# A decode kernel's output written as two single-row transfers on two queues, and its MLP bias loaded in two pieces

## The chip, the cores and the metric

The kernel runs on one core of a Trainium2 chip. The metric is the device time of one execution in microseconds (us); before the change the median of three runs is 134.12 us. Profiles show one execution each; their span (132.1 us here) is counted from the first to the last instruction and is a little shorter than the device time.

## The reference

One decoding step for two sequences (B = 2, one token each, width 576): attention over a window of the last 2048 cached positions, and beside it an MLP with squared ReLU. Both start from the same layer-normed input, and both are added to the input. The MLP's own x is not used.

```python
def _A_ref(x, k_cache, v_cache, wq, wo):          # 32 query heads, 16 KV heads, head size 128
    W = min(4096, max(256, Sk // 4))              # 2048 of 8192 positions
    q = (x @ wq).reshape(B, Sq, Hq, Dh)...
    k = jnp.repeat(k_cache[:, :, Sk - W:, :], rep, axis=1)
    v = jnp.repeat(v_cache[:, :, Sk - W:, :], rep, axis=1)
    p = _softmax(jnp.einsum("bhqd,bhkd->bhqk", q, k) * (Dh ** -0.5))
    o = jnp.einsum("bhqk,bhkd->bhqd", p, v)
    return o... @ wo                              # 4096 -> 576

def _B_ref(x, w1, b1, w2, b2):                    # 576 -> 4608 -> 576
    h = jnp.einsum("bsd,df->bsf", x, w1) + b1
    r = jnp.where(h > 0, h, 0)
    return jnp.einsum("bsf,fd->bsd", r * r, w2) + b2

xn = _layernorm(A_x)
return A_x + _A_ref(xn, ...) + _B_ref(xn, ...)    # (2, 1, 576), bf16
```

## The kernel before

The sync engine's queue loads K, V and all large weights, one transfer after another. The scalar engine's queue loads the input x, the two biases, and writes the output. All that is to be summed (input, second bias, attention times wo, MLP times w2) is accumulated by matmuls in one PSUM tile, `out_ps`. The 576 columns of the result stand there as four quarters of 144 columns, quarter q of sequence b on partition 32 q + 16 b, which gives eight partitions with data.

```python
    BS = 16
    MB = BS * (B - 1) + 1                # 17
    RM = 32 * (NG4 - 1) + MB             # 113
    OQ = D // 4                          # 144
    W2P = [(9, 15), (15, 17), (17, 18)]  # pieces of the last part of w2
    R9 = 9
    HW = L1 // NG4                       # 576
    ...
    xb_sb = const.tile([B + 1, D], BF16, name="xb_sb")
    nc.scalar.dma_start(out=x_sb, in_=x2d)
    ...
    load_k(0)                            # all on the sync queue
    wq_sb = issue_flat(A_wq, "wq")
    load_k(1); load_v(0); load_k(2); load_v(1); load_k(3)   # one per line in the kernel
    ...
    b1_sb = const.tile([2 * NG4, HW], BF16, name="b1_sb")   # 8 rows of 576
    ...
    softmax(0)
    load_v(2)
    b1_rows = B_b1.rearrange("(x n) -> x n", n=HW)
    for i0, i1 in ((0, 2), (2, 4), (4, 6), (6, 8)):
        nc.scalar.dma_start(out=b1_sb[i0:i1, :], in_=b1_rows[i0:i1, :])
    nc.scalar.dma_start(out=xb_sb[B:B + 1, :], in_=B_b2.rearrange("(o n) -> o n", o=1))
    step(1)
    ...
    mlp_h(w1_sb)                         # uses b1_sb
    wo_sb = issue_flat(A_wo, "wo")
    ...
    nc.sync.dma_start(out=w2a_sb[:], in_=w2_rows[0])
    nc.sync.dma_start(out=w2b_sb[:], in_=w2_rows[1, :, 0:R9 * D])
    for r0, r1 in W2P:
        nc.sync.dma_start(out=w2c_sb[:, (r0 - R9) * D:(r1 - R9) * D], in_=w2_rows[1, :, r0 * D:r1 * D])
    step(NU - 1)
    pv_all(NU - 2)
    pv_all(NU - 1)
    ...                                  # out_ps += wo, w2a parts
    for r in range(FR):                  # FR = 18
        w, o = (w2b_sb, r) if r < R9 else (w2c_sb, r - R9)
        out_acc(hT_sb[:, 1, r, :], w, o, stop=(r == FR - 1))

    fin_sb = work.tile([RM, OQ], BF16, tag="fin", name="fin_sb")
    out_v = out2d.rearrange("b (q n) -> q b n", q=4)
    nc.scalar.dma_start(out=out_v, in_=w2b_sb[0:RM:BS, 0:OQ])   # early, of no meaning
    nc.scalar.copy(out=fin_sb[:], in_=out_ps[:])
    nc.scalar.dma_start(out=out_v, in_=fin_sb[0:RM:BS, :])      # the output
```

The first of the two output transfers writes weights, which the second overwrites. It serves to have a transfer of this form run once before the one that counts. The framework orders the two by a semaphore.

Of the kernel before, what the change touches and what calls it, by code (L numbers as in the profile page):

```python
# [16 lines left out]
def kernel(  # L17
# [14 lines left out]
    nc = tc.nc  # L32
    P = 128
    B, Sq, D = A_x.shape
# [43 lines left out]
    BS = 16  # L78
    MB = BS * (B - 1) + 1
    RM = 32 * (NG4 - 1) + MB  # L80
    OQ = D // 4
# [18 lines left out]
    out2d = out.rearrange("b s d -> (b s) d")  # L100
# [79 lines left out]
    for t0, half, k0, n, pc in ((0, 0, 0, NK, 0), (0, 1, 0, NK, 1), (1, 0, 1, NK - 1, 1), (1, 1, 0, NK - 1, 0)):  # L180
# [11 lines left out]
                          in_=own[:].unsqueeze(2).to_broadcast([P, NC, WC]))  # L192
# [11 lines left out]
                          in_=ident[0:2 * NG4, 0:2 * NG4].rearrange("p (x g) -> p x g", g=NG4).unsqueeze(3)  # L204
# [209 lines left out]
    softmax(0)  # L414
    load_v(2)
    b1_rows = B_b1.rearrange("(x n) -> x n", n=HW)
    for i0, i1 in ((0, 2), (2, 4), (4, 6), (6, 8)):
        nc.scalar.dma_start(out=b1_sb[i0:i1, :], in_=b1_rows[i0:i1, :])
    nc.scalar.dma_start(out=xb_sb[B:B + 1, :], in_=B_b2.rearrange("(o n) -> o n", o=1))
    step(1)  # L420
# [16 lines left out]
    w2b_sb = kvpool.tile([P, R9 * D], BF16, tag="kv", name="w2b")  # L437
# [13 lines left out]
        out_acc(hT_sb[:, 1, r, :], w, o, stop=(r == FR - 1))  # L451

    fin_sb = work.tile([RM, OQ], BF16, tag="fin", name="fin_sb")
    out_v = out2d.rearrange("b (q n) -> q b n", q=4)
    nc.scalar.dma_start(out=out_v, in_=w2b_sb[0:RM:BS, 0:OQ])
    nc.scalar.copy(out=fin_sb[:], in_=out_ps[:])  # L456
    nc.scalar.dma_start(out=out_v, in_=fin_sb[0:RM:BS, :])


# [28 lines left out]
```

## Time and profile before

| | us |
|---|---|
| device time, median of 3 runs (133.97 to 134.12) | 134.12 |
| span of the profiled execution | 132.1 |
| TensorE matmul busy | 84.6 (64%) |
| VectorE busy | 63.2 (48%) |
| ScalarE busy | 46.7 (35%) |
| bytes read from memory | 53.62 MB, 406 GB/s over the span |

How to read it: busy shares are of the whole span. An engine at 64% can still wait most of the time in one stage and be the limit in another, so the stages are what counts. "PEld" is TensorE's weight load, "ACTq" and "SPq" are the queues on which the scalar and the sync engine issue transfers, and `L457` is a line of the kernel. The time of an issuing instruction is not the transfer's time: the transfer starts after it and has landed when its semaphore has all its increments.

The DMA queues of the whole execution (packets, bytes, share of the 16 DMA engines' time), of which q1 is the sync engine's and q10 the scalar engine's, and the small transfers that this change is about:

```profile
q1 hardware_dynamic: 3456, 53.61, 95.2%
q10 hardware_dynamic: 46, 0.02, 0.1%
...
b_sb<-in_B_b_dram ACTq DMA_DIRECT2D x4, 2.2 KB
...
out_dram<-w2b ACTq DMA_DIRECT2D x1, 2.2 KB
out_dram<-fin_sb ACTq DMA_DIRECT2D x1, 2.2 KB
```

### The profile page before, as it was taken

How to read it: one execution, taken by the hardware profiler on the slowest of the kernel's cores; microseconds unless marked ns; L12 is line 12 of the kernel's file. 1: busy time of each engine (PE TensorE's matmuls, PEld its weight loads, DVE VectorE, ACT ScalarE, POOL GpSimd, SP SyncE). 2: the span in 40 equal slices, each digit the busy share in tenths (PEclk: the TensorE clock that was granted, in tenths of full speed). 3: DMA queues.
4: the chain of work that ended last, by engine and by line, in shares of the span. 5: the costliest groups of instructions: out<-in, count | busy, mean ns of one | idle time of the engine just before them, and what ended most of it. 6: DMA issues, size and time to landing. Idle time of an engine off the chain costs nothing.

```text
span 132.1 us, 2285 instructions
## 1 busy us (share of the span) xinstructions
PE 84.6 (64%) x949; PEld 52.6 (40%) x949; DVE 63.2 (48%) x176; ACT 46.7 (35%) x67; POOL 4.9 (4%) x15
## 2 busy tenths in 40 slices
PE   0089319599589687697599787104819972739471
PEld 0069202286345353363455443002417640229360
DVE  7764400344557677396547687410075667550000
ACT  5725400339566085283256094200106632000000
POOL 5000000010010100100100100100000001000000
PEclk9999955959999999999779999855695999555955
DMA  4999899999999999999999999999999999899960
GB/s 160 397 437 526 369 388 442 422 432 432 429 432 422 442 417 427 437 432 437 432 427 414 437 488 402 445 424 405 427 427 442 468 435 458 376 408 418 418 255 1
DMA packets 3511, 53.76 MB, mean 407 GB/s; under 512 B 419, under 2 KB 558, under 8 KB 814
## 3 DMA queue, kind: packets, MB, share of 16 engines
q1 hardware_dynamic: 3456, 53.61, 95.2%
q8 instruction: 7, 0.11, 0.3%
q10 hardware_dynamic: 46, 0.02, 0.1%
q14 instruction: 2, 0.02, 0.0%
HBM read 53.62 MB, written 0.00 MB: 406 GB/s over the span
## 4 chain that ended last, share of the span: by engine, by line
DMA 78%; PE 15%; ACT 2%; SPq 1%; DVE 1%; issue 1%; ACTq 0%; DVEq 0%
DMA w<-in_B_w_dram 25%; DMA w2c<-in_B_w_dram 24%; DMA k<-in_A_k_cache_dram 16%; DMA wq<-in_A_wq_dram 13%; PE kT_ps L97 5%; PE h_ps L94 3%; PE q_ps L94 3%; PE sc_ps L94 2%; PE out_ps L94 1%; PE o_ps L94 1%; ACT kT L270 1%; DVE qrow L238 1%; SPq L106 0%; ACT qrow L238 0%; DVE qz L254 0%
## 5 line engine op out<-in xcount | busy, mean ns | idle before, releaser
L97 PE MATMUL kT_ps<-ident_f,k 128*128 128x128 f32 x256 | 41.4, 312 | 5.7 <-DMA k<-in_A_k_cache_dram 3.9
L97 PEld LDWEIGHTS kT_ps<-ident_f,k 128*128 128x128 f32 x256 | 32.9, 161 | 18.8 <-issue 9.9
L270 ACT COPY kT<-kT_ps 128x1024 bf16<-128x1024 bf16 x32 | 31.9, 1012 | 17.8 <-PE kT_ps L97 17.8
L272 DVE COPY kT<-kT_ps 128x1024 bf16<-128x1024 bf16 x32 | 21.8, 682 | 6.4 <-PE kT_ps L97 6.1
L94 PE MATMUL sc_ps<-kT,qz 128*32 128x512 bf16 x128 | 9.9, 388 | 6.7 <-DVE kT L272 4.7
L302 ACT ACTIVATE p<-sc_ps,bias 128x512 bf16<-128x512 f32 x8 | 5.5, 688 | 21.4 <-DVE gown L298 18.2
L94 PE MATMUL o_ps<-v,pT 128*32 128x512 bf16 x128 | 11.2, 429 | 0.0
L94 PEld LDWEIGHTS <-xnT 128*4 128x4 bf16 x108 | 3.5, 121 | 16.8 <-issue 15.2
L94 PE MATMUL h_ps<-w,xnT 128*4 128x288 bf16 x72 | 4.3, 429 | 8.0 <-DMA w<-in_B_w_dram 8.0
L305 DVE STREAM_TRANSPOSE pT<-p 128x512 bf16<-128x512 bf16 x8 | 5.7, 710 | 6.2 <-ACT p L302 6.2
L335 DVE SCALAR_TENSOR_TENSOR o<-o_ps,in_s,o 128x128 f32<-128x128 f32 x24 | 8.3, 345 | 0.4
L291 DVE TENSOR_REDUCE m<-sc_ps 128x1 f32<-128x512 f32 x8 | 5.5, 692 | 4.8 <-PE sc_ps L94 4.8
L375 DVE TENSOR_TENSOR hrow<-t 100x1152 bf16<-100x1152 f32 x2 | 2.6, 1355 | 9.6 <-ACT t L373 9.6
L94 PE MATMUL q_ps<-wq,xnT 128*4 128x512 bf16 x36 | 4.0, 627 | 4.9 <-DMA wq<-in_A_wq_dram 4.9
L295 POOL PARTITION_ALL_REDUCE gmax<-m x8 | 2.9, 367 | 104.9 <-DVE m L293 104.9
L94 PE MATMUL op_ps<-o,of_h 128*32 128x129 f32 x16 | 3.7, 316 | 4.6 <-DVE o L335 4.6
L456 ACT CAST fin_sb<-out_ps 113x144 bf16<-113x144 f32 x1 | 0.3, 280 | 17.9 <-PE out_ps L94 17.9
L94 PEld LDWEIGHTS <-qz 128*32 128x32 bf16 x128 | 2.1, 94 | 10.4 <-DVE kT L272 7.2
L97 PE MATMUL pro_ps<-ident,xn_sb 2*128 2x2 bf16 x5 | 0.9, 182 | 6.8 <-DVE xn_sb L171 6.5
L94 PEld LDWEIGHTS <-hT_sb 128*17 128x17 bf16 x144 | 3.4, 108 | 3.6 <-issue 3.5
L94 PE MATMUL out_ps<-wo,ws 128*17 128x144 bf16 x128 | 4.0, 325 | 1.2 <-DVE ws L351 1.2
L238 DVE CAST qrow<-q_ps 100x512 bf16<-100x512 f32 x1 | 0.7, 692 | 8.2 <-PE q_ps L94 8.2
(71 smaller groups left out, 57.4 us busy)
## 6 DMA issues: line engine op xcount, KB each, us to landing
k<-in_A_k_cache_dram SPq DMA_DIRECT2D x8, 2048.0 KB, 21.0
v<-in_A_v_cache_dram SPq DMA_DIRECT2D x8, 2048.0 KB, 21.5
w<-in_B_w_dram SPq DMA_DIRECT2D x1, 5184.0 KB
wq<-in_A_wq_dram SPq DMA_DIRECT2D x1, 4608.0 KB, 17.8
wo<-in_A_wo_dram SPq DMA_DIRECT2D x1, 4608.0 KB
w2a<-in_B_w_dram SPq DMA_DIRECT2D x1, 2592.0 KB, 26.9
w2b<-in_B_w_dram SPq DMA_DIRECT2D x1, 1296.0 KB
w2c<-in_B_w_dram SPq DMA_DIRECT2D x1, 864.0 KB
```

The costliest lines, as they stand in the source:

```text
L94: tc.keep_in_program_order(nc.tensor.matmul(*a, **k))
L97: tc.keep_in_program_order(nc.tensor.transpose(*a, **k))
L238: cp(out=qrow[:, k * QW:(k + 1) * QW].rearrange("p (i a d) -> p i a d", a=2, d=Dh), in_=q_ps[0:RB, k * QW // 2:(k + 1) * QW // 2].rearrang ...
L270: nc.scalar.copy(out=kT, in_=kT_ps[:])
L272: nc.vector.tensor_copy(out=kT, in_=kT_ps[:])
L291: nc.vector.tensor_reduce(out=m1[:], in_=sc_ps[:], axis=AX.X, op=ALU.max)
L295: nc.gpsimd.partition_all_reduce(gmax[:], m2[:], channels=P, reduce_op=ReduceOp.max)
L302: nc.scalar.activation(out=p_sb[:], in_=sc_ps[:], func=ACT.Exp, bias=bias[:, 0:1], scale=scale, accum_out=o1[:, Dh:Dh + 1])
L305: nc.vector.transpose(out=pT[:].rearrange("p j r -> p (j r)"), in_=p_sb[:])
L335: nc.vector.scalar_tensor_tensor(scalar=in_s[:, k:k + 1], in1=o1[:, 0:Dh], op0=ALU.mult, op1=ALU.add, **kw)
L375: nc.vector.tensor_tensor(out=h4[:, :, k * HB:(k + 1) * HB], in0=t4, in1=t4, op=ALU.mult)
L456: nc.scalar.copy(out=fin_sb[:], in_=out_ps[:])
```

## The change

The output is written as two transfers of one row (one sequence) each, four partitions of 144 columns, one on the scalar queue and one on the sync queue. The early transfer is split in the same way, so that each queue again has had a transfer of the same form before the one that counts. The purpose is to let two engines issue the two halves side by side, each with a simpler pattern. Apart from that the first MLP bias is loaded in two transfers of four rows instead of four of two rows, which spares the scalar queue two issues.

```diff
-    for i0, i1 in ((0, 2), (2, 4), (4, 6), (6, 8)):
+    for i0, i1 in ((0, 4), (4, 8)):
         nc.scalar.dma_start(out=b1_sb[i0:i1, :], in_=b1_rows[i0:i1, :])
...
     fin_sb = work.tile([RM, OQ], BF16, tag="fin", name="fin_sb")
-    out_v = out2d.rearrange("b (q n) -> q b n", q=4)
-    nc.scalar.dma_start(out=out_v, in_=w2b_sb[0:RM:BS, 0:OQ])
+    out_v = out2d.rearrange("b (q n) -> b q n", q=4)
+    queues = (nc.scalar, nc.sync)
+    for b in range(B):
+        queues[b].dma_start(out=out_v[b], in_=w2b_sb[BS * b:RM:32, 0:OQ])
     nc.scalar.copy(out=fin_sb[:], in_=out_ps[:])
-    nc.scalar.dma_start(out=out_v, in_=fin_sb[0:RM:BS, :])
+    for b in range(B):
+        queues[b].dma_start(out=out_v[b], in_=fin_sb[BS * b:RM:32, :])
```

## The prediction, made before the changed kernel ran

> **What bounds the kernel now.** I read the page's slices first. The DMA row says 4999899999999999999999999999999999899960: from the second slice to the last but two the sixteen DMA engines are busy nine tenths or more in all slices but two. The stages agree (columns: stage, length, busy time and instructions of each engine, clock, DMA share, GB/s):
>
> ```profile
> 33.00:91.00 58.00, 39.54 (x355) 22.38 (x354) 34.70 (x87) 25.99 (x36) 2.20 (x6) 0.92 1.00 430
> 91.00:127.90 36.90, 24.46 (x429) 16.07 (x429) 14.74 (x36) 6.79 (x12) 0.37 (x1) 0.73 0.99 422
> 127.90:132.05 4.15, 1.34 (x36) 1.03 (x35) 0.00 (x0) 0.28 (x1) 0.00 (x0) 0.50 0.05 19
> ```
>
> Up to 127.9 us the kernel is one saturated stream of 53.6 MB, and nothing that the change touches there is bytes. What can move is the last 4.15 us, in which the transfers idle (0.05). Therefore I read next the chain of work that ended last, its end:
>
> ```profile
> 96.70 0.04 issue
> 96.74 31.12 DMA w2c<-in_B_w_dram
> 127.86 0.04 issue
> 127.90 1.36 PE out_ps L94 x36
> 129.27 0.02 issue
> 129.29 0.28 ACT fin_sb L456
> ```
>
> and the timeline of the same stretch (start, length, engine, line):
>
> ```profile
> 125.80 0.65 ACTq L455 DMA_DIRECT2D out_dram<-w2b  x1
> ...
> 127.90 1.34 PE L94 MATMUL out_ps<-w2c,hT_sb 128*17 128x144 bf16 x36 [0.82 <-DMA w2c<-in_B_w_dram]
> 127.91 1.14 PEld L94 LDWEIGHTS <-hT_sb 128*17 128x17 bf16 x35 [1.03 <-issue]
> 129.29 0.28 ACT L456 CAST fin_sb<-out_ps 113x144 bf16<-113x144 f32 x1 [17.85 <-PE out_ps L94]
> 129.60 0.54 ACTq L457 DMA_DIRECT2D out_dram<-fin_sb  x1
> ```
>
> The chain merges 36 matmuls that really wait for three slivers of w2c. In the single records the last four start at 128.95, after the last sliver's sixteenth semaphore step at 128.91. The 1.36 us are therefore still transfer time, and the bare tail begins at 128.91. From there, by the single records of instructions, DMA packets and semaphore steps: matmuls and their wait to 129.27, cast 129.29 to 129.57, issue of the output 129.60 to 130.145 (0.543), first output packet at 130.79 (0.645 after the issue ended), last packet at 130.88, last semaphore step at 131.22 (0.34 later), then the closing barriers to 132.06 (0.84). The waits of the sync engine show the same as one number, the wait for the final output at the kernel's end (total, times, longest):
>
> ```profile
> SPq L483 <- DMA out_dram<-fin_sb: 2.3, 1, 2.3
> SPq L483 <- DMA out_dram<-w2b: 0.3, 1, 0.3
> ```
>
> The change can shorten only 129.57 to 131.22, 1.65 us, 1.2% of the kernel. This alone makes a move over 2% most unlikely.
>
> **What the Trainium skill says.** "DMA: Bandwidth & Descriptors", section "Issuing engines are not separate DMA queues": transfers from the scalar and the sync engine run on the same 16 engines and interleave, and a second issuer saves only issue time. The records agree: the early output's packets of the scalar queue stand between w2c's of the sync queue at 127.09 to 127.81. So two queues bring no bandwidth here, and 2.2 KB need none.
>
> Same page, "Why a DMA increments its semaphore by 16 and not by 1": the number of engines comes from the slowest dimension, and the issuer adds the remaining steps at once. The trace agrees: the output shows eight packets of 288 bytes and four semaphore packets, that is four engines, and one early step at 130.57 ahead of four. A row as four pieces should again use four engines, with one piece each.
>
> Same page, "Two DMAs through the same engine are not ordered": a later transfer to the same bytes must wait for the earlier one's semaphore. The kernel's program agrees: ahead of the final issue the scalar queue has a wait (129.30) on the semaphore of the early output, which had its last step at 128.25, 1.35 us before it was needed.
>
> **Part one, the final output.** It removes one issue with a pattern of three dimensions (4 x 2 x 144) and adds two with two dimensions (4 x 144), one on each queue, side by side. What does a dimension cost? Per issue, in this trace: K and V loads, whose source has three (32 x 4 x row), have a median of 0.535 us; w2 and wo loads, with two, 0.33 to 0.43; the bias transfers on the scalar queue, rows alone, 0.25 to 0.31; the present output, three, 0.543. I take 0.31 for the scalar half and 0.36 for the sync half: 0.543 - 0.31 = **0.23 us** saved on the scalar queue. The sync half starts later by one hop across engines; hops show as 0.02 to 0.06 us "issue" pieces in the chain, so 0.05, and ends at 129.60 + 0.05 + 0.36 = 130.01 against 130.145: **0.13 us** saved. The later one counts.
>
> Then the time between the issue's end and the early semaphore step: 0.42 us in both outputs now, but 0.18 in the bias transfers, which have fewer pieces. If the step is a fair sign of how long the descriptors take, the first packet also comes up to 0.24 us sooner; the single-row x load, first packet 0.38 us after its issue, points the same way against 0.645. I book half, **0.12 us**, since four pieces lie between two and eight and the two queues may wait for one another there. Per engine one packet of 288 bytes less goes through each queue, 0.016 us, and with both queues in use the engine sees as many as before: nothing. Receipt of 0.34 us and closing barriers of 0.84 us stay. Sum: 0.13 + 0.12 = **0.25 us**, with 0.1 to 0.45 as its likely extent.
>
> **Part two, the early transfers.** The scalar one is issued at 125.80 as now and brings half the pieces. The sync one waits for w2b as well (last step 125.78) and lies in the sync rings behind the rest of w2c. It touches four engines, probably those on which the present one ran. Its packets show two of these served at 127.09 to 127.15 and two at 127.72 to 127.81, right after a sliver's semaphore packet. The slowest six engines only end their w2c packets near 128.4 and land between 128.69 and 128.91, so the four seem not to be among them. Even at the slowest, 128.4 plus some 0.5 us to landing is 128.9, 0.7 us before the sync queue needs it at 129.6. Cost on the path: **0**.
>
> **Part three, the bias.** Four issues of 0.25 to 0.31 us at 4.43 to 5.71 become two, some 0.6 us less of the scalar queue. In that time the scalar engine loads a table (4.34 to 5.62), so even the square root at 5.64 gains next to nothing, and xnT waits for wq until 19.2. The bias is used only at 82.7. **0** again. A side effect: the eight DMA semaphores go round, so v_0 at 8.05 waited for k_0, and k_2, v_1 and k_3 at 10.52, 13.39 and 16.21 each for a bias piece. With two pieces fewer, two loads are issued earlier. But the rings then still hold wq and k_1, which land at 19.2 and 24.0, and in 8 to 33 us the share is 0.98: earlier issue makes a longer queue and no earlier byte. Eight row packets of 51 ns with their semaphore packets lay on two engines, now on four: 0.12 us either way at most, if one of them were the slowest.
>
> **The rivals.**
> - *The sync half becomes the last to land* because the early sync transfer is late behind w2c and the final one waits for it. For it: same rings, and the wait is really in the program. Against it: the 0.7 us just worked out. If it happened, the final sync issue would slip, say by 0.5 us: 134.3 to 134.5.
> - *The saving is only issue time, and descriptor work of both queues is one behind the other.* For it: the 0.645 us has no counterpart of this form in the trace. Then one half gains 0.23 and the other loses it again: 134.0 to 134.15, no difference to be seen in three runs that spread by 0.15.
> - *The queue lag shrinks wholly with the pieces.* For it: 0.18 against 0.42. Then 0.13 + 0.24 and a little more: 133.7.
> - *Something in the stream moves* through the changed order of early issues or through different sharing between engines. A stream of 127 us needs to change by only 0.2% to hide all of the above. Nothing in the profile names a direction; I widen the range for it.
>
> **How the range and the chances follow.** 134.12 - 0.25 = 133.87; the third rival is somewhat likelier than the second, since both signs of lag point one way, so I say **133.8 us**. The range of 133.4 to 134.2 has at its lower end 0.45 us of tail plus 0.25 of stream, and at its upper end no gain and half the spread. Two per cent are 2.7 us, more than the whole tail that the change touches: faster by 2% 0.01, slower by 2% 0.01, within 0.98. I think a real gain under 2% about three times in four.
>
> **What would show each step.** The two final issues should last 0.25 to 0.45 us each rather than 0.54 and start within 0.1 us of one another and of the cast's end. The sync engine's wait at the end for the output should shrink from 2.3 us. From the cast's end to the span's end, now 2.48 us, I expect 2.15 to 2.3. The last w2c landing should be at 128.9 give or take 0.2, with the DMA row as full as before. I am wrong if the sync half's final issue starts late (the first rival), if both issues still last 0.54, or if the chain's w2c piece ends elsewhere by more than the tail gained.

## The result, and the profile after

| | before | after |
|---|---|---|
| device time, median of 6 runs each | 134.05 us (133.85 to 134.19) | 134.39 us (134.34 to 134.51) |
| ratio, with 95% interval | | 1.0028 (1.0015 to 1.0041) |
| span of the profiled execution | 132.1 us | 132.5 us |

The changed kernel is slower by 0.28%, some 0.35 us. The loss is small but clear of noise: its fastest run lies above the slowest of the kernel before. I had predicted 133.8 us and a range that ended at 134.2.

First the stream. The page's slices of the changed kernel, DMA row, and then the stages (columns as in the prediction):

```profile
DMA  4999999999999999999999999999999999899950
```

```profile
33.00:91.00 58.00, 39.56 (x356) 22.39 (x355) 34.60 (x87) 26.11 (x36) 2.20 (x6) 0.92 1.01 430
91.00:128.02 37.02, 24.32 (x429) 16.16 (x429) 14.75 (x36) 6.79 (x12) 0.37 (x1) 0.73 0.99 422
128.02:132.47 4.45, 1.28 (x36) 1.02 (x35) 0.00 (x0) 0.28 (x1) 0.00 (x0) 0.88 0.05 17
```

The transfers are as full as before, at the same 430 and 422 GB/s. The stage after them has grown from 4.15 to 4.45 us. The chain of work that ended last, its end:

```profile
96.69 31.33 DMA w2c<-in_B_w_dram
128.02 0.04 issue
128.06 1.31 PE out_ps L94 x35
129.37 0.02 issue
129.39 0.28 ACT fin_sb L458
```

The chain's piece of w2c ends at 128.02 instead of 127.86 and the last one lands at 129.06 instead of 128.91, but the cast starts only 0.10 us later than before (129.39 against 129.29). The timeline of the last stretch (start, length, engine, line):

```profile
125.95 0.66 SPq L457 DMA_DIRECT2D out_dram<-w2b  x1
125.96 0.61 ACTq L457 DMA_DIRECT2D out_dram<-w2b  x1
...
129.39 0.28 ACT L458 CAST fin_sb<-out_ps 113x144 bf16<-113x144 f32 x1 [18.04 <-PE out_ps L94]
129.69 0.57 SPq L460 DMA_DIRECT2D out_dram<-fin_sb  x1
129.70 0.52 ACTq L460 DMA_DIRECT2D out_dram<-fin_sb  x1
```

Both final issues start within 5 ns of each other, right after the cast. So the split does what it was meant to do. But neither is shorter to speak of: 0.52 and 0.57 us where the one issue took 0.54. What the sync queue waited for (total, times, longest):

```profile
SPq L460 <- DMA out_dram<-w2b: 2.1, 1, 2.1
SPq L486 <- DMA out_dram<-fin_sb: 1.1, 2, 0.8
SPq L460 <- ACT fin_sb L458: 1.0, 1, 1.0
```

The wait for the sync queue's early store is over 1.0 us before the cast is done; that one is hidden. The wait at the end is now shared between the sync engine's own issue and two landings, so its 1.1 cannot be compared with the 2.3 of before. The single records of DMA packets and semaphore steps give the rest (us from the span's start; the early step is the one that comes ahead of the landings of the data):

| | before, one store | after, scalar half | after, sync half |
|---|---|---|---|
| end of the issue | 130.145 | 130.219 | 130.261 |
| early semaphore step | 130.568 | 130.641 | 130.998 |
| first packet | 130.790 | 130.865 | 131.229 |
| from the issue's end to the first packet | 0.645 | 0.646 | 0.968 |
| last landing | 131.220 | 131.272 | 131.635 |

The scalar half behaves as the whole store did. The sync half's packets come 0.364 us after the scalar half's, with idle DMA engines in between. The delay is already there in the early step, which came 0.42 us after the scalar half's issue and 0.74 us after the sync half's; from that step to the first packet both took the same 0.22 to 0.23 us. So the sync half waited between the end of its issue and that step. From the cast's end to the last landing the tail was 131.220 - 129.572 = 1.65 us and is now 131.635 - 129.668 = 1.97 us: 0.32 us of the 0.41 by which this span is longer. The other 0.10 is the later cast. To the span's end it is 2.80 us, where I had expected 2.15 to 2.3.

### The profile page after: what moved, and what is told of

Same layout as the page of the kernel before. It is cut to its first block, busy times and chain, and to the rows that moved or that the text cites. A ratio compares the mean times of both kernels' runs of the same rounds, so it can differ in the third digit from the quotient of the medians.

```text
span 132.5 us, 2287 instructions
## 1 busy us (share of the span) xinstructions
PE 84.2 (64%) x949; PEld 52.2 (39%) x949; DVE 63.1 (48%) x176; ACT 46.6 (35%) x67; POOL 4.9 (4%) x15
## 4 chain that ended last, share of the span: by engine, by line
DMA 78%; PE 15%; ACT 2%; SPq 1%; DVE 1%; issue 1%; ACTq 0%; DVEq 0%
DMA w<-in_B_w_dram 25%; DMA w2c<-in_B_w_dram 24%; DMA k<-in_A_k_cache_dram 16%; DMA wq<-in_A_wq_dram 13%; PE kT_ps L97 5%; PE h_ps L94 3%; PE q_ps L94 3%; PE sc_ps L94 2%; PE out_ps L94 1%; PE o_ps L94 1%; ACT kT L270 1%; DVE qrow L238 1%; SPq L106 1%; ACT qrow L238 0%; DVE qz L254 0%
## 5 line engine op out<-in xcount | busy, mean ns | idle before, releaser
L97 PEld LDWEIGHTS kT_ps<-ident_f,k 128*128 128x128 f32 x256 | 32.4, 159 | 19.5 <-issue 10.0
```

Source lines behind the costliest of these rows:

```text
L97: tc.keep_in_program_order(nc.tensor.transpose(*a, **k))
```

## The experiments

Three theories: **A**, two stores share a path between issue and first packet, and the second waits there for the first; **B**, the sync queue is by itself that slow for a store; **C**, the stream of loads was disturbed by the bias part. "Tail" below is the time from the cast's end to the output's last landing, from the single records.

### Each part alone

```diff
 bias_only: the kernel before, with
-    for i0, i1 in ((0, 2), (2, 4), (4, 6), (6, 8)):
+    for i0, i1 in ((0, 4), (4, 8)):
 split_only: the changed kernel, with that line put back
```

> Output as in the kernel before, only the bias comes in two transfers. Theory A (the two final stores share one path from issue to first packet, and the second comes 0.36 us after the first): the bias has no part in the loss, 134.05 us give or take 0.1, last landing of w2c near 128.9 us, final store as before (first packet 0.65 us after the issue's end). Theory B (the sync queue by itself takes longer from a store's issue to its first packet, 0.97 us): the same 134.05. Theory C (the stream of loads was disturbed by fewer bias transfers and the earlier issues that follow): some 134.2, last landing of w2c near 129.05.

> Output split as in the changed kernel, the bias in four transfers as before. Theories A and B: the whole loss stays, 134.35 us give or take 0.1, and the sync half's first packet comes about 0.36 us after the scalar half's. Theory C: only the part of the loss that lies behind the last load stays, 134.2 or a little more, with the last landing of w2c back at 128.9 us.

Measured: bias_only 134.22 us against 134.12 for the kernel before beside it, ratio 1.0008 (0.9998 to 1.0017), tail 1.65 us. split_only 134.64 us, ratio 1.0037 (1.0023 to 1.0050), tail 1.97 us, the sync half's first packet 0.364 us after the scalar half's (131.443 and 131.079). The last landing of w2c was 129.13 in the one and 129.21 in the other, both later than the 128.91 of before, so it doesn't follow the bias. By itself bias_only came out as theory C had said (134.2, last load near 129.05). But split_only, with the bias as before, should then have had its last load back at 128.9 and a smaller loss, and had neither. The 0.32 us of the tail are with the output, and theory C falls as their cause. A loss of some 0.1 us by the bias part is neither shown nor excluded.

split_only lost more than the changed kernel did, 0.52 us against 0.34. In its profile the last load landed 0.15 us later and the barriers that close the kernel took 1.00 us instead of 0.83. What moves these two is open. In the profiles of all the kernels here the barriers took 0.82 to 1.09 us, so the tail says more of the output than a difference of 0.2 us between two times.

### Each half alone

```diff
 sync_half:
-    for b in range(B):
+    for b in (1,):
         queues[b].dma_start(out=out_v[b], in_=fin_sb[BS * b:RM:32, :])
 scalar_half: the same with (0,)
```

One row of the output is left out in each.

> The changed kernel without the final transfer of sequence 0 on the scalar queue; that row keeps the early transfer's weights. So the sync half is alone. Theory A: its first packet comes 0.65 us after the end of its issue instead of 0.97, and the time falls by some 0.3 us to 134.05 to 134.15. Theory B: still 0.97 us, time 134.35 to 134.4. Theory C says nothing on the lag, and that 0.1 to 0.15 us over the kernel before stay.

> The changed kernel without the final transfer of sequence 1 on the sync queue; that row keeps the early transfer's weights. So the scalar half is alone. Theories A and B: issue 0.52 us and 0.65 us to the first packet as in the changed kernel, because it was first there, last landing 0.35 us sooner than with the sync half, 134.05 us give or take 0.1. Theory C: 134.15 to 134.2. Against all three: under 133.9, if half the pieces made the store quicker after all.

| | time, us | ratio (95%) | issue's end to first packet | tail |
|---|---|---|---|---|
| sync half alone | 134.19 | 1.0004 (0.9995 to 1.0014) | 0.647 | 1.63 |
| scalar half alone | 134.13 | 1.0006 (0.9995 to 1.0016) | 0.651 | 1.60 |

Alone, the sync half has the same lag as any other store. Theory B falls, and A stands: the 0.32 us arise only where both are there. The second thing to see is that half the pieces bring almost nothing. The tail of a half is 0.01 to 0.05 us shorter than that of the whole store, although it has four pieces instead of eight. So the gain that I had booked was not there to be had.

### How long the path is held, and by what

```diff
 both_scalar:    queues = (nc.scalar, nc.scalar)
 columns_split:  each queue stores 72 of the 144 columns of all eight pieces
 two_pieces:     final sync store: out_v[1, 0:2] <- fin_sb[BS:BS + 33:32, :] (half of that row is left out)
 staggered:      fin_w = copy of fin_sb by the vector engine; sync store reads fin_w
```

> The changed kernel with both rows on the scalar queue, one issue after the other. Theory A as the halves alone leave it: a store holds the shared path some 0.33 us, and a store that finds it free has its first packet 0.65 us after its issue's end. The second issue ends over 0.5 us after the first, so it finds the path free: lag 0.65 us for both, last landing later than with one store by one issue and its gap, some 0.55 us, time 134.6 to 134.75. Theory A2 (any second store in flight costs 0.33 us, however far behind the first): second lag 0.97 us, time 134.9 to 135.1.

> Two stores on two queues as in the changed kernel, but split by columns: each has eight pieces of 72 elements instead of four of 144. If the path is held per piece, the second store's first packet comes some 0.65 us after the first store's and the time is near 134.75 to 134.9. If it is held per store, or per DMA engine used (four both times), the gap stays 0.33 to 0.36 us and the time 134.4 to 134.6.

> The changed kernel with the final sync store cut to two of its four pieces (the other half of that row keeps the early transfer's weights). Held per piece or per engine used by the store that comes second: the sync store's first packet comes 0.17 to 0.25 us after the scalar store's, time 134.25 to 134.35. Held by the first store, which still has four pieces, or a fixed time per store: the gap stays 0.33 to 0.36 us, time 134.4 to 134.6.

> The changed kernel, but the sync store reads a copy of the result that the vector engine makes after the scalar engine's cast, so that its issue starts some 0.2 us after the scalar store's instead of beside it. Theory A (the first store holds a path that both need, the second waits for it to come free): the gap between the two first packets stays near 0.36 us, and so do the last landing and the time, 134.3 to 134.5. Theory A2 (a second store in flight always costs its 0.33 us on top): gap near 0.56, time 134.5 to 134.7. Theory A3 (only issues within some nanoseconds collide): gap near 0.2 us, time 134.2 to 134.3.

| | time, us | ratio (95%) | second issue starts after first | gap of the first packets | tail |
|---|---|---|---|---|---|
| split_only (for comparison) | 134.64 | 1.0037 (1.0023 to 1.0050) | 0.00 | 0.364 | 1.97 |
| both_scalar | 134.67 | 1.0042 (1.0030 to 1.0054) | 0.62 | 0.623 | 2.23 |
| columns_split | 134.43 | 1.0028 (1.0018 to 1.0038) | 0.00 | 0.270 | 1.89 |
| two_pieces | 134.40 | 1.0025 (1.0014 to 1.0036) | 0.00 | 0.364 | 1.91 |
| staggered | 134.72 | 1.0038 (1.0024 to 1.0053) | 0.23 | 0.363 | 1.97 |

The timeline of staggered:

```profile
129.90 0.28 ACT L458 CAST fin_sb<-out_ps 113x144 bf16<-113x144 f32 x1 [17.23 <-PE out_ps L94]
130.21 0.52 ACTq L462 DMA_DIRECT2D out_dram<-fin_sb  x1
130.21 0.20 DVE L460 COPY fin_w<-fin_sb 113x144 bf16<-113x144 bf16 x1 [11.70 <-ACT fin_sb L458]
130.44 0.57 SPq L462 DMA_DIRECT2D out_dram<-fin_w  x1
```

This is the clearest of the four: the sync issue starts 0.23 us late, and its first packet still comes 0.363 us after the scalar store's. The sync issue also took 0.05 us longer, so without any wait the gap would have been 0.28, which is what a collision of simultaneous issues alone (A3) gives; a fixed extra cost (A2) gives some 0.6. What was measured fits theory A: the first store holds something for 0.36 us, and a second one that comes within that time waits for the rest. In both_scalar the second came later than that and had its usual 0.654 us from issue to packet. The gap doesn't grow with the pieces: it is the same when the second store has two instead of four, and smaller when both have eight shorter ones with a third dimension. That last point I had not expected and leave open. staggered's time is higher than its tail explains: its last load landed at 129.51, later than in any run so far, for which I have no cause.

One observation doesn't fit. In the profiles of both halves, of columns_split and of staggered the two early stores, also issued within 5 ns and of the same stepped form, had their first packets 0.02 to 0.03 us apart; in those of the changed kernel, split_only and two_pieces 0.20 to 0.28. The early step shows the same: 0.39 to 0.43 us after the issue's end in the former, 0.51 to 0.64 in the latter, and there for both stores, not only for the second. Where w2c's packets still run, the path is not always held. What decides it is open.

### Two views on the tail

```diff
 vector_cast: kernel before, with  nc.vector.tensor_copy(out=fin_sb[:], in_=out_ps[:])
 no_early:    kernel before, without the early store
```

> The kernel before with the cast of the result on the vector engine instead of the scalar engine, which takes from the bare tail rather than from the stores. The scalar engine's cast took 0.28 us; the vector engine's cast of 100x512 of the same types took 0.69, so 113x144 should take some 0.2 us, and the hop to the scalar queue is no longer than now. 0.05 to 0.1 us less in the tail from last load to last landing, time 133.95 to 134.1.

> The kernel before without the early store. In the trace before, the early store's issue took 0.645 us and the final one's 0.543, with the same 0.64 us to the first packet. If the early one is what makes the second quicker, the final issue now takes some 0.65 us and the time rises by 0.1 to 134.15 or 134.2. If it was only the busy transfers around it that made the early one slower, the issue stays at 0.54 and the time at 134.05.

vector_cast: the cast took 0.308 us, not 0.2, against 0.280 on the scalar engine; 134.19 us, ratio 1.0000 (0.9986 to 1.0014). No gain; scaling down from a wider cast missed a fixed part. no_early: the final issue took 0.644 us instead of 0.543, as expected if the early store serves the later one, tail 1.74 us instead of 1.65; 134.23 us, ratio 1.0009 (0.9999 to 1.0019). The 0.1 us is seen in the records; the times alone can't show it.

### Why the issue takes 0.52 us and not 0.31

The four-row bias transfers of the changed kernel took 0.265 and 0.308 us, the four-piece stores twice that. Three kernels with small added transfers on the scalar queue ask why. Their times, of one run each (135.17, 134.27 and 134.25 us), say little; in forms the load of k_1 had to wait for a small transfer's semaphore and was issued at 16.4 us instead of 2.2, and it landed at 25.5 instead of 24.0.

```diff
 forms:  + load 4x144 (out of one row of x, into every 32nd partition), load 4x288 (out of rows of wq,
         into neighbouring partitions), store 4x144 (from every 32nd), store 2x576
 forms2: + loads 4x144, 4x240, 4x256, 4x288 out of rows of wq into 4 neighbouring partitions,
         + store 2x2x288 from every 16th partition
 forms3: + loads 4x144 out of rows of wq into partitions 4:8, 0:113:32 and 0:8:2,
         + stores 4x144 from partitions 0:4 and 0:113:32
```

> The kernel before with four small transfers added on the scalar queue in the first 20 us: a load of 4x144, a load of 4x288 out of longer rows, a store of 4x144 and a store of 2x576; the first two fill a tile that nothing reads, the stores are overwritten at the end. They ask why the issue of 4x144 took 0.52 us where I took 0.31 from loads. If a store costs more to issue than a load, both stores take some 0.5 us or more and both loads 0.25 to 0.35. If short pieces cost more, the two with 288 bytes per piece take 0.5 and the others 0.3. The time of one look says little, 134 to 135.

> The kernel before with five small transfers added early on the scalar queue: loads of four pieces out of longer rows with 288, 480, 512 and 576 bytes per piece into a tile that nothing reads, and one store of 2x2x288 (four pieces of 576 bytes, three dimensions), overwritten at the end. They ask which property of a transfer makes its issue 0.52 to 0.6 us and its first semaphore step 0.42 us later, instead of 0.26 and 0.18. If it is the length of the piece, 288 and 480 bytes are slow and 576 is quick, the store with them. If it is the third dimension, all four loads are quick and the store slow. If it is that one side is one unbroken run cut into four, all five are quick. The first issue of the kernel after x may be slow for being early, as 0.61 us was in the look before. Time of one look 134 to 135.5.

> The kernel before with five small transfers of 4x144 added early on the scalar queue: loads out of longer rows into partitions one after another, into every 32nd and into every second partition (a tile that nothing reads), and stores from partitions one after another and from every 32nd (overwritten at the end). If a step between the partitions is what makes an issue 0.5 to 0.6 us and its first step 0.42 us late, then both with step 32 and the load with step 2 are slow and the two others take 0.26 and 0.18. If the unbroken run on the memory side is needed for it, all loads are quick and both stores slow or only the stepped one. Time of one look 134 to 135.

In forms the store of two whole rows from partitions 0 and 1 was issued in 0.27 us (last line), the store of four pieces in 0.59. So a store as such is not slow.

```profile
1.39 0.61 ACTq L140 DMA_DIRECT2D pad<-in_A_x_dram  x1
6.81 0.26 ACTq L143 DMA_DIRECT2D pad<-in_A_wq_dram  x1
...
8.62 0.59 ACTq L141 DMA_DIRECT2D out_dram<-k  x1
20.08 0.27 ACTq L142 DMA_DIRECT2D out_dram<-k  x1
```

In forms2 the four loads with pieces of 288 to 576 bytes took 1.32 us together, 0.27 to 0.34 each. So the length of a piece isn't the cause, which had been my best guess. The store of 2x2x288, with long pieces, was slow:

```profile
1.39 1.32 ACTq L139 DMA_DIRECT2D pad<-in_A_wq_dram  x4
...
9.27 0.63 ACTq L141 DMA_DIRECT2D out_dram<-k  x1
```

forms3 settles it. The loads (first three lines) differ in nothing but their partitions: neighbours, every 32nd, every second. The stores (last two) are of 4x144 from neighbours and from every 32nd:

```profile
1.40 0.27 ACTq L139 DMA_DIRECT2D pad<-in_A_wq_dram  x1
1.70 0.61 ACTq L140 DMA_DIRECT2D pad<-in_A_wq_dram  x1
2.34 0.64 ACTq L141 DMA_DIRECT2D pad<-in_A_wq_dram  x1
...
8.79 0.28 ACTq L142 DMA_DIRECT2D out_dram<-k  x1
9.60 0.58 ACTq L143 DMA_DIRECT2D out_dram<-k  x1
```

A step between the partitions doubles the issue of these small transfers, in loads and in stores. It isn't the only thing that goes with a long issue: the K and V loads, on neighbouring partitions, took 0.535 us on the sync queue, and the load of x, two rows on neighbouring partitions and the first on the scalar queue, took 0.556. The early semaphore step, the sign that I had used for the lag, goes with it: 0.17 and 0.18 us after the issue's end for neighbours, 0.42 to 0.43 for stepped ones. The output of this kernel stands on every 16th partition, and each half of it on every 32nd, because the four column groups of the matmul put it there. The split couldn't change that.

### Stores without a step

```diff
 four_stores: BS = 1 (both sequences on neighbouring partitions); four final stores of 2x144,
              out_v[q] <- fin_sb[32 * q:32 * q + B, :], two per queue, one early store per queue
 two_banks:   quarters 0, 1 of the result in one PSUM bank, 2, 3 in another; two casts on the scalar and
              two on the vector engine into fin_sb[0:17, 0:576]; row b stored from partition 16 b,
              one row per queue; input and second bias are added after the attention
 one_store:   the same with BS = 1 and one store of 2x576 on the scalar queue
```

> The kernel before with the two sequences on neighbouring partitions and the output in four stores of 2x144, each from two neighbouring partitions, two per queue, one early store per queue. If the step between partitions is the cost: issues of 0.26 to 0.33 us, first step 0.18 us after them; the second pair's issue ends near 0.6 us after the cast where the one store's ended 0.57 after it, and its first packets come 0.2 us sooner than now unless the pairs hold one another up on the shared path; time 133.85 to 134.05. If each of four stores holds the path 0.36 us as before: the last landing 0.8 us or more later than now, time 134.7 to 135.0. If the step is not the cost: issues of 0.52 each, time 134.7 or more.

> What the looks at single transfers point to: stores without a step between partitions. The four quarters of the result stand in two PSUM banks, two each; the scalar and the vector engine cast them, two casts each, into one row of 576 per sequence, on partitions 0 and 16; each queue stores one row from one partition, with early stores of the same form. Two casts instead of one on each engine: 0.15 to 0.3 us more. Issue 0.26 instead of 0.54, first packet 0.48 us after it instead of 0.645, and the second store only some 0.03 us behind the first as in four_stores, because only stepped patterns hold the shared path for 0.36 us: 0.45 us less. Receipt 0.34 to 0.47. From the last load's landing to the last landing of the output 0.1 to 0.3 us less than in the kernel before (2.31), time 133.8 to 134.0 if the stream of loads ends where it did. If the path is held 0.36 us per store whatever its form, no gain: 134.1 to 134.2.

> The same casts, but the two sequences on neighbouring partitions and one store of 2x576 on the scalar queue, with one early store of that form. No second store, so nothing to wait for on the shared path. Issue 0.26 to 0.28, first packet 0.48 after it; from the last load's landing to the output's last landing as in two_banks give or take 0.05. In four_stores, the other kernel with neighbouring partitions, the stream of loads ended 1.0 us later; if that comes from this layout the time is near 134.8, if not, 133.8 to 134.0.

| | time, us | ratio (95%) | last load landed | last load to output's last landing |
|---|---|---|---|---|
| kernel before | | | 128.91 | 2.31 |
| four_stores | 135.16 | 1.0084 (1.0071 to 1.0098) | 129.94 | 2.31 |
| two_banks | 135.11 | 1.0073 (1.0057 to 1.0088) | 129.68 | 2.43 |
| one_store | 134.93 | 1.0064 (1.0049 to 1.0079) | 129.81 | 2.30 |

Issues took 0.25 to 0.29 us, and the first packets came 0.47 to 0.56 us after the issue's end instead of 0.645. Two unstepped stores issued together had their first packets 0.03 and 0.10 us apart in the two pairs of four_stores and 0.08 in two_banks, so there is no hold of 0.36 us here. These stores also have one or two pieces instead of four, and no pair of four-piece stores without a step was tried; which of the two ends the hold is not shown. That much worked. But in four_stores the second pair of stores uses up what the first gains, and in two_banks two casts on an engine take 0.55 to 0.62 us where one took 0.28. No end is shorter by more than 0.02 us. And in all three the stream of loads ended 0.8 to 1.0 us later.

### Where the stream lost up to a microsecond

two_banks had put its result tile where the kernel before has a smaller unused one, ahead of all large tiles, which moved these by 576 bytes per partition. Two runs take that apart:

```diff
 two_banks_placed: two_banks with fin_sb in the place of another tile of the same size; large tiles as before
 more_pad: the kernel before, with
-    const.tile([P, 144], F32, name="pad_0")
+    const.tile([P, 288], F32, name="pad_0")
     (and fin_sb in the place of another tile, to make room)
```

> As two_banks (quarters in two banks, four casts, two unstepped stores), but the tile of the result takes no new room ahead of the large tiles, so K, V and the weights land at the addresses in SBUF where the kernel before has them. If the 576 bytes by which two_banks moved them made its stream of loads end 0.8 us later, the last load now lands near 129.0 to 129.2 us and the time is 134.1 to 134.35, since the tail (2.43 us from there to the output's last landing in two_banks, 2.31 in the kernel before) stays. If the two banks themselves or the row stores slow the stream: 134.8 to 135.2 again.

> The kernel before with the unused tile at the start of SBUF 576 bytes per partition larger, so all large tiles lie 576 bytes further on (the result's tile takes the place of another small one to make room). Nothing else changes. If the place in SBUF sets the pace of the stream: last load near 129.7 us, time 134.7 to 135.0. If not: 134.05 give or take 0.1.

The end of the chain in more_pad, to be held against 127.86 and 127.90 in the kernel before:

```profile
97.58 31.16 DMA w2c<-in_B_w_dram
128.74 0.04 issue
128.78 1.40 PE out_ps L94 x34
```

more_pad: 134.88 us, ratio 1.0058 (1.0046 to 1.0071), last load 129.81, tail 1.66 us as before. So with 576 bytes of displacement and the output as before the stream ended 0.9 us later. two_banks_placed: 134.47 us, ratio 1.0030 (1.0018 to 1.0042), last load back at 129.03, 0.65 us sooner than in two_banks. The two pairs agree that the place matters. How much of the 0.9 us it makes is less sure: in staggered, where no large tile moved, the stream also ended 0.60 us later than before, and the load of w1 landed at 91.62 us there, against 91.67 in more_pad and 91.05 before.

two_banks_placed shows the new end without that burden, in its timeline the casts and the two stores:

```profile
129.44 0.62 DVE L462 CAST fin_sb<-out_b 17x144 bf16<-17x144 f32 x2 [11.66 <-PE out_b L94]
129.46 0.55 ACT L462 CAST fin_sb<-out_ps 17x144 bf16<-17x144 f32 x2 [18.44 <-PE out_b L94]
130.14 0.26 SPq L464 DMA_DIRECT2D out_dram<-fin_sb  x1
130.14 0.24 ACTq L464 DMA_DIRECT2D out_dram<-fin_sb  x1
```

The issues are half as long as in the changed kernel, but they start 0.45 us later, and the output lands 2.42 us after the last load against 2.31 before. The expectation for its time was too low, because the closing barriers also took 0.99 us after the last landing instead of 0.84, within what they took in other profiles. In four_stores and one_store the small tiles ahead of the large ones shrink with BS, so the same cause may be at work there; that wasn't tried. None of the eighteen kernels is faster than the kernel before.

## Why the prediction was wrong

**What bounds the kernel**: right. The stream ran as before and the change touched the tail alone. That the effect stays under 2% followed from it.

**Part one, the issue (0.13 us booked)**: the step that failed was "0.543 - 0.31". It took the bias transfers as the measure for a store with two dimensions. forms3 shows that the number of dimensions was the wrong property for these stores: with two dimensions in all five transfers, the step between the partitions made the difference, and the halves have one as the whole had. Measured instead: 0.52 and 0.57 us, so the later issue ended 0.59 us after the cast, 0.02 later than the single one had. The trace before already spoke against a price per dimension. I had listed w2 and wo, with two dimensions, at 0.33 to 0.43 us, and left out wq and w1 (`w`), which come from the same line of the kernel with the same form:

```profile
1.41 0.57 SPq L119 DMA_DIRECT2D wq<-in_A_wq_dram  x1
58.00 0.58 SPq L119 DMA_DIRECT2D w<-in_B_w_dram  x1
95.41 0.34 SPq L119 DMA_DIRECT2D wo<-in_A_wo_dram  x1
```

Why these differ is open.

**Part one, the lag (0.12 us booked)**: I read the bias transfers' shorter lag as that of fewer pieces. In forms3, with four pieces each time, the early step came 0.17 to 0.18 us after the issue without a partition step and 0.42 to 0.43 with one. The load of x, my second sign, is two rows on neighbouring partitions and not a single row; it too has no step. With half the pieces the lag was 0.646 us as before, and with the other half in front of it 0.968. This term alone turns the sign: not -0.12 but +0.32.

**The rivals**: the second, "descriptor work of both queues is one behind the other", was the right mechanism. I sized it at 0.23 us, to be cancelled by an equal gain of the issue. The wait was 0.32 and the gain was nil, so it came to a loss of 0.32 rather than to no difference. I had not given it the weight it deserved: the trace before held no two small transfers issued together, so nothing in it spoke against the wait. The Trainium skill's "DMA: Bandwidth & Descriptors", "Issuing engines are not separate DMA queues", says that a second issuer saves only issue time. For stepped stores at the end of this kernel it didn't save even that: the two issues ran side by side, and the time came back behind them.

**Part two, the early stores**: right. The sync one landed at 128.70, I had worked out 128.9, and the final one waited another 1.0 us for the cast (first rival refuted).

**Part three, the bias**: no effect on the time that can be measured (bias_only, 1.0008 with an interval across 1), and the earlier issues did as worked out: in the changed kernel v_0 was issued at 2.68 instead of 8.05 us, and landed at 28.9 in both.

**The last rival**, "something in the stream moves", was too vague to be of use. The last load landed at 128.91 before, at 129.06 in the changed kernel and at 128.96 to 129.21 in the nine others from bias_only to no_early (staggered aside), with and without the split; a part of the 0.35 us may lie there.

## What to carry to other kernels

Take the cost of a small transfer from one with the same access pattern, the step between partitions included, and not from one of the same size. Don't count on a small transfer at the end of a kernel getting quicker by being cut in two on two queues: here, with a partition step, the second half waited a third of a microsecond behind the first, and each half alone was within 0.05 us as slow as the whole. When a layout changes, look whether large tiles have moved, before a slower stream is put down to the thing that was tried.

## What the runs showed of the hardware

- In small transfers of one to eight pieces on the scalar queue, a step between the partitions went with an issue of 0.52 to 0.65 us instead of 0.24 to 0.34, in loads and stores, for steps of 2, 16 and 32 alike, with pieces of 288 bytes or 576. In forms3, where only the partitions differ, the first semaphore step came 0.42 to 0.43 us after the issue's end instead of 0.17 to 0.18. An exception is the load of x, the first on its queue: 0.556 us without a step.
- The second of two such stores issued together at the end of the kernel had its first packet 0.36 us after the first's (0.27 in one form), and the wait lay between the end of its issue and its early semaphore step. The early stores, issued while w2c's packets still ran, were only 0.02 to 0.03 us apart in four profiles and 0.20 to 0.28 in three. Two stores without a step, with one or two pieces, were 0.03 to 0.10 us apart.
- With the K, V and weight tiles moved by 576 bytes per partition in SBUF the stream of 53.6 MB ended 0.9 us later (128.91 to 129.81). Which tile and which address matter wasn't tried, and one kernel lost 0.60 us of its stream with no large tile moved.
- Without an early store of the same form ahead of it, the final store took 0.1 us longer to issue (0.644 in no_early against 0.543).
